# An mLSTM scan with a gated MLP: every store on SyncE's queue, and another order of work ahead of the first step

## The chip, the cores and the metric

The kernel runs on one core of one Trainium2 chip. The metric is the device time of one execution in microseconds (us); lower is better. The median of the runs shown stands for the kernel. Beside them there is one profiled execution, from which all durations below are read.

## What is computed

The inputs are q, k, v and an output gate of shape (4, 8, 768, 40), and an input and a forget gate of shape (4, 8, 768): 4 batches, 8 heads, 768 positions, 40 features. The reference is a stabilised recurrence over the positions, followed by a two-layer MLP:

```python
for t in range(S):
    m_new = np.maximum(f_gate[:, :, t] + m, i_gate[:, :, t])
    f_stab = np.exp(f_gate[:, :, t] + m - m_new)
    i_stab = np.exp(i_gate[:, :, t] - m_new)
    C = f_stab * C + i_stab * einsum('bhd,bhe->bhde', v[t], k[t])
    n = f_stab * n + i_stab * k[t]
    y[t] = sigmoid(o_gate[t]) * einsum('bhde,bhe->bhd', C, q[t]) / max(|n.q[t]|, 1)
x = y as (3072, 320)
h = x @ w_in                      # (320, 2048)
out = (h * sigmoid(h)) @ w_out    # (2048, 320)
```

(The indices are shortened here.) Everything is in 32-bit floats; the two weights come in as 64-bit words.

## The kernel before, in words

**Units.** The recurrence is cut into 12 chunks of 64 positions. A unit (class `Unit`) is one chunk of two batches, all heads: 24 units, numbered in the order of time, two for each chunk. A unit computes 64 by 64 scores of q and k (`scores`, L511), multiplies them with a matrix of decay factors in tile D (`weigh`, L538), applies them to v (`values`, L567, or `near_values` and `far_values`, L583 and L598), adds what earlier chunks left in the state Cm, and updates the state: `keys` (L530) multiplies k by the last decay factors, `state` (L648) multiplies that with v, `carry` (L666 for the first chunk, L668 and L674 later) adds it to Cm. The result is divided by its norm (`norm`, `level`, L611 to L621), multiplied by the output gate (`gate` makes the tanh, L488; `scale`, L635, makes tile x), transposed on TensorE (`xpose`, L690) and put into the MLP's input (`xput`, L696 to L702).

**Steps.** Three units make a step of 384 tokens (class `Step`): 8 steps. A step runs over 16 blocks of 128 hidden features, fc = 0 to 15. `mm1(fc)` is x times w_in (L743, tile ph); `act(fc)` makes the gated value: a tanh on ScalarE (L750, tile th), a product on VectorE (L764), and in steps 1 to 7 a split into two parts (gh on ScalarE, L769; gl on VectorE, L773). `mm2(fc)` adds that block's product with w_out (L794) into three accumulators `pout`, one for each 128 tokens. `mm2` runs two blocks behind `mm1`, so the last two blocks of a step run beside blocks 0 and 1 of the next one. After the last `mm2` of each accumulator `store` (L804 to L818) evicts it on ScalarE (L814, tile ob) and issues two DMAs of 64 rows each to the output (L818).

**Order.** All engines run a hand-written order: what stands first in the program is issued first on its engine, and every engine and DMA queue is in order. In each step the three units of the next one are worked into the blocks: unit u starts at block 2, 7 or 12 (`PLACES`). At that block TensorE runs the unit's matmuls after `mm1` (`block`), one block later `turn` transposes its x and issues the loads of a later unit on SyncE's queue: D, qk, ko, vb (L430 to L451) and lq (L464).

**Queues.** Loads go through SyncE's queue. A store goes through SyncE's queue in steps 0 and 1 and for the first half of each store of the last step, and through ScalarE's queue in all other cases (L817). Two writes of the running log-decay to a scratch tensor LFd go through ScalarE's queue (`spread`, L185).

**Ahead of the first step.** Units 0, 1 and 2 are computed by an order of their own (L857 to L955): the gate recurrence for the first two chunks on VectorE, the decay factors of these units by matmuls (`mask`, `expo`, `reach`) and exponentials on ScalarE, then scores, values, state and x of each. Beside it, weights are loaded in pieces, `Part`: i0 to i7 (256 columns of w_in, its first 256 rows), c0 to c6 (512 columns of w_in's last 64 rows), o0 to o7 (256 rows of w_out). `wmake` turns a piece from 64-bit words into 32-bit floats by two ScalarE passes (L259, L260) and one on VectorE (L261) and then issues the load of a later piece. `halve` (L274) splits a c piece: for each of two halves, a copy on ScalarE (L280) and a subtraction (L281), on VectorE unless another engine is named. In step 0 the table `FILL` adds work after each block: the rest of the weights' pieces, unit 3's remainder, and the rest of the gate recurrence. Unit 3's first work on GpSimd is `near` (L495), a product that waits for its qk.

Of the kernel before, what the change touches and what calls it, by code (L numbers as in the profile page):

```python
# [8 lines left out]
F32 = mybir.dt.float32  # L9
# [5 lines left out]
ALU = mybir.AluOpType  # L15
# [3 lines left out]
B, H, S, D = 4, 8, 768, 40  # L19
L = 64  # L20
# [3 lines left out]
DM = H * D  # L24
# [4 lines left out]
NT = UPS * UT  # L29
NSTEP = NU // UPS  # L30
# [13 lines left out]
def mlstm_mlp_kernel(  # L44
# [113 lines left out]
    def gates(lo, hi):  # L158

        init = NEG if lo == 0 else m_t[:, lo - 1 : lo]  # L160
        nc.vector.tensor_tensor_scan(
            m_t[:, lo:hi], f_t[:, lo:hi], i_t[:, lo:hi], init, op0=ALU.add, op1=ALU.max
        )
        yield
        l1 = max(lo, 1)
        tt = nc.vector.tensor_tensor
        tt(out=f_t[:, l1:hi], in0=f_t[:, l1:hi], in1=m_t[:, l1 - 1 : hi - 1], op=ALU.add)
        yield
        tt(out=f_t[:, l1:hi], in0=f_t[:, l1:hi], in1=m_t[:, l1:hi], op=ALU.subtract)
# [46 lines left out]
    class Part:  # L216
# [54 lines left out]
                nc.vector.tensor_copy(wi[self.lo], full)  # L271
            self.full = full

        def halve(self, eng=None):  # L274
            K, n, full = self.K, self.n, self.full
            for k in range(2):
                a, b = slice(k * K, (k + 1) * K), slice((1 - k) * K, (2 - k) * K)
                cs = slice(k * n, (k + 1) * n)
                hi = self.hi[a, :, cs]
                nc.scalar.copy(hi, full[a])  # L280
                (eng or nc.vector).tensor_tensor(  # L281
                    out=self.hi[b, :, cs], in0=full[a], in1=hi.bitcast(F32), op=ALU.subtract
                )

    def split_out(i):

# [31 lines left out]
        )  # L318


    order = "i0 c0 i1 o0 i2 c2 o1 i3 o2 c4 i4 o3 i5 o4 c6 i6 o5 i7 o6 o7"
    parts = [part(x[0], int(x[1])) for x in order.split()]
    nload, nmade = [0], [0]

    def halve(i, eng=None):
        next(p for p in parts if p.nm == f"c{i}").halve(eng)

    def wload(n):
        for p in parts[nload[0] : nload[0] + n]:
            p.load()  # L330
        nload[0] = min(nload[0] + n, len(parts))

    def wmake(n):

        for p in parts[nmade[0] : nmade[0] + n]:
            p.make()
            wload(1)
        nmade[0] = min(nmade[0] + n, len(parts))
# [16 lines left out]
    def couple(name):  # L355

        return psP.tile([128, H, 128], F32, tag="p", name=name)

    class Unit:


        def __init__(self, n):
            self.n, self.c, self.p = n, n // NP, n % NP


        def mask(self, to=None):
# [120 lines left out]
        def gate(self):  # L487
            nc.scalar.activation(self.ot, self.ot, AF.Tanh, scale=0.5)  # L488

        def look(self):  # L490
            nc.scalar.activation(self.lq, self.lq, AF.Exp)  # L491

# [28 lines left out]
            self.last = p2.tile([128, H], F32, tag="last", name=f"last{self.n}")  # L521
            nc.scalar.copy(self.last, self.Dm[:, :, L - 1])

        def keys(self):
            last = getattr(self, "last", None)
            if last is None:
                last = self.Dm[:, :, L - 1]
            if self.c < NC - 1:
                self.kw = p2.tile([128, H, D], F32, tag="kw", name=f"kw{self.n}")
                nc.vector.tensor_tensor(  # L530
                    out=self.kw,
                    in0=self.kt,
                    in1=last.unsqueeze(2).broadcast_to([128, H, D]),
                    op=ALU.mult,
                )
# [80 lines left out]
            nc.vector.reciprocal(den, den)  # L616
            self.den = den

        def level(self):
            y = self.po[:, :, :D]  # L620
            nc.vector.tensor_tensor(  # L621
                out=y, in0=y, in1=self.den.unsqueeze(2).broadcast_to([128, H, D]), op=ALU.mult
            )

        def scale(self):
            n, y = self.n, self.po[:, :, :D]
# [3 lines left out]
            for to, e in (  # L630
                (xf[:, : H * DA].rearrange("p (h e) -> p h e", e=DA), slice(0, DA)),
                (rest[:, 0], slice(DA, D)),
                (rest[:, 1], slice(DA, D)),
            ):
                nc.vector.scalar_tensor_tensor(  # L635
                    out=to, in0=self.ot[:, :, e], scalar=1.0, in1=y[:, :, e],
                    op0=ALU.add, op1=ALU.mult,
                )
# [67 lines left out]
    class Step:  # L706
# [97 lines left out]
        def store(self, t):  # L804
            n = self.j * UPS + t
            c, p = n // NP, n % NP
            if self.j < NSTEP - 1:
                ob = p3.tile([128, DM], F32, tag="ob", name=f"ob{n}")
            else:
                ob = pb.tile([128, DM], F32, tag="big", name=f"ob{n}")  # L810
            if self.j == NSTEP - 1 and t == UPS - 1:
                nc.vector.tensor_scalar(ob, self.po[t], 0.5, None, op0=ALU.mult)
            else:
                nc.scalar.activation(ob, self.po[t], AF.Copy, scale=0.5)  # L814
            for k in range(2):
                r = (2 * p + k) * S + c * L
                q = nc.sync if self.j in (0, 1) or self.j == NSTEP - 1 and k == 0 else nc.scalar  # L817
                q.dma_start(out[r : r + L, :], ob[k * L : (k + 1) * L])  # L818


# [55 lines left out]
    for _ in range(2):  # L876
# [4 lines left out]
    run(5, gates(0, L))  # L881
    thirds(0)
    widen()
    run(5, gates(L, 2 * L))
# [4 lines left out]
    u0.scores()  # L889
    warm(1)  # L890
    u0.mask()
    u0.expo()
    u0.expo_act()
    u1.mask()
    u1.expo()
    u1.expo_act()
    u0.keys()
    u0.weigh()
    u2.reach()
    u2.reach_act()  # L900
    u0.gate()
    u2.mask()
    u2.expo()
    u2.expo_act()
    u2.keep()
    u2.near()
    warm(1)
    u1.scores()
    u1.keys()
    u1.weigh()  # L910
    u0.place()
    u0.values()
    u0.state()
    u0.carry()
    u1.gate()
    u0.norm()
    u0.level()
    u2.scores()
    u2.weigh()
    u1.place()  # L920
    u1.values()
    u2.place()
    u2.values()
    u2.gate()
    u0.scale()
    u1.norm()
    u1.level()
    u2.norm()
    u2.level()
    u2.scale()  # L930
    u1.scale()
    wmake(2)
    steps[0] = st = Step(0)
    u2.keys()
    u0.xpose()
    u1.state()
    u1.carry()
    u3.reach()
    u3.mask(couple("e3")[:, :4, :].rearrange("p b (c t) -> p (b c) t", t=L))
    u3.expo()  # L940
    u2.room(psU, "u")
    u2.xpose()
    u1.xpose()
    u0.xput(st)
    halve(0, nc.gpsimd)
    u2.xput(st)
    u1.xput(st)
    u3.load_qk()
    u3.load_kvo()
    u2.state()  # L950
    u3.reach_act()
    u3.near()
    run(5, two)
    wmake(1)
    u3.expo_act()  # L955
    FILL = {
        0: lambda: (run(1, near), wmake(1), u2.carry(), u3.gate(), u3.keys()),
        1: lambda: (wmake(1), u3.scores(), u3.weigh(), u4.load_qk(), u4.load_kvo()),
        2: lambda: (wmake(2), run(2, near), u4.load_d(), u4.load_q(), u4.shift()),
        3: lambda: (halve(2), wmake(1), u4.add(), run(1, late[0])),  # L960
# [34 lines left out]
    for j in range(NSTEP):  # L995
        st = steps[j]
# [105 lines left out]
```

## Time and profile before

| | us |
|---|---|
| median of 3 runs | 464.67 (464.63 to 466.96) |
| the profiled execution, device time | 465.99 |
| its span, first to last instruction | 464.1 |
| TensorE's matmul busy in it | 445.1 |
| first `mm1` of step 0 starts | 23.93 |
| `mm1(2)` of steps 2, 3, 4, 5, 6, 7 starts | 144.28, 196.51, 253.11, 307.83, 361.56, 414.85 |

A row of the timeline gives the start in us from the span's start, the duration, the engine, the line, the operation, the tile written and those read, shapes, the number of like instructions merged into the row, and in brackets how long the engine was idle before it and what ended that. PE is TensorE's matmul, PEld its weight load, DVE is VectorE, ACT ScalarE, POOL GpSimd, SP SyncE; a q behind a name is that engine's queue of DMA issues. A row of the windows view gives a stretch, its length, then for each engine its busy time in it and the number of instructions, then TensorE's granted clock (1.00 is full speed), the DMA engines' busy share and GB/s. In the waits view a row gives who waited for whom, the total, how often, and the longest.

### The profile page before, as it was taken

The page shows a single profiled execution, that of the slowest core. Times are in us where ns is not written, and L with a number is a line of the kernel's source. Part 1 is how long each engine was busy: PE and PEld are TensorE (multiplying, and loading weights), DVE is VectorE, ACT ScalarE, POOL GpSimd, SP SyncE. Part 2 cuts the span into 40 slices and gives each one's busy share as a digit, 9 for nine tenths or more (in the row PEclk, how much of TensorE's full clock was granted, in tenths as well). Part 3 has the DMA queues.
Part 4 walks back from the last instruction along what each step waited for, and adds up shares of the span by engine and source line. Part 5 has one row for each costly group of instructions (what it writes and reads, how often), then busy time and mean ns, then how long its engine had stood idle before and what let it go on. Part 6 is the DMA issues. An engine that isn't in the chain of part 4 may idle for free.

```text
span 464.1 us, 11033 instructions
## 1 busy us (share of the span) xinstructions
PE 445.1 (96%) x4477; PEld 408.8 (88%) x4477; DVE 269.8 (58%) x609; ACT 212.1 (46%) x442; POOL 115.6 (25%) x123
## 2 busy tenths in 40 slices
PE   7899999999999999979999899998999899999995
PEld 3667677899999999979999799998999799998995
DVE  5777799578775566444664555636655355533342
ACT  6674856444753442525424344434344344333332
POOL 4224234134142234131431332322332311000000
PEclk9899999999999999998999999999999999998999
DMA  8999896361331442141430522413313200001001
GB/s 211 320 295 274 235 265 148 97 159 49 81 122 40 127 122 65 59 110 56 124 101 22 148 63 76 123 48 118 122 31 93 62 1 2 2 12 32 0 1 42
DMA packets 27314, 47.03 MB, mean 101 GB/s; under 512 B 4160, under 2 KB 14464, under 8 KB 27264
## 3 DMA queue, kind: packets, MB, share of 16 engines
q1 hardware_dynamic: 24224, 43.45, 33.6%
q10 hardware_dynamic: 3040, 2.89, 2.3%
q8 instruction: 35, 0.57, 0.5%
q14 instruction: 15, 0.12, 0.1%
HBM read 42.30 MB, written 4.01 MB: 100 GB/s over the span
## 4 chain that ended last, share of the span: by engine, by line
PE 83%; DMA 6%; DVE 3%; ACTq 3%; ACT 2%; issue 1%; SPq 0%; DVEq 0%
PE ph L743 37%; PE pout L794 35%; DMA wro<-in_w_out_dram 3%; ACTq L818 3%; PE p L598 3%; DMA qk<-in_qk_dram 3%; PE p L511 2%; PE pu L648 2%; PE p L583 2%; PE p L690 2%; ACT ob L814 1%; ACT th L750 1%; DVE th L764 1%; DVE D L538 1%; PE pt L193 0%
## 5 line engine op out<-in xcount | busy, mean ns | idle before, releaser
L750 ACT ACTIVATE th<-ph 128x384 f32<-128x384 f32 x128 | 62.4, 487 | 139.8 <-PE ph L743 132.7
L764 DVE SCALAR_TENSOR_TENSOR th<-th,ph 128x384 f32<-128x384 f32 x112 | 62.1, 555 | 107.5 <-ACT th L750 106.9
L743 PE MATMUL ph<-xh,wh 128*128 128x384 f32 x336 | 116.3, 346 | 0.0
L743 PE MATMUL ph<-xl,wh 128*128 128x384 f32 x336 | 114.6, 341 | 0.0
L794 PE MATMUL pout<-woh,gh 128*128 128x320 f32 x336 | 106.5, 317 | 2.2 <-ACT ob L814 2.2
L794 PE MATMUL pout<-woh,gl 128*128 128x320 f32 x336 | 104.2, 310 | 0.0
L794 PE MATMUL pout<-wol,gh 128*128 128x320 f32 x336 | 103.7, 308 | 0.0
L773 DVE TENSOR_TENSOR gl<-th,gh 128x384 fp32r<-128x384 f32 x112 | 64.6, 577 | 47.5 <-ACT gh L769 47.5
L769 ACT CAST gh<-th 128x384 fp32r<-128x384 f32 x112 | 57.5, 513 | 74.9 <-DVE th L764 74.3
L743 PE MATMUL ph<-xh,wl 128*128 128x384 f32 x224 | 76.6, 342 | 0.0
L794 PEld LDWEIGHTS pout<-woh,gh 128*128 128x128 f32 x336 | 63.6, 189 | 5.5 <-ACT ob L814 3.4
L495 POOL TENSOR_TENSOR qt<-qk,lq 104x512 f32<-104x512 f32 x22 | 29.5, 1340 | 141.5 <-ACT lq L491 125.0
L743 PEld LDWEIGHTS ph<-xl,wh 128*128 128x128 f32 x336 | 63.8, 190 | 0.2
L743 PEld LDWEIGHTS ph<-xh,wh 128*128 128x128 f32 x336 | 63.7, 190 | 0.2
L794 PEld LDWEIGHTS pout<-wol,gh 128*128 128x128 f32 x336 | 63.5, 189 | 0.0
L794 PEld LDWEIGHTS pout<-woh,gl 128*128 128x128 f32 x336 | 63.5, 189 | 0.0
L668 POOL TENSOR_TENSOR Cm<-Cm,lq 40x328 f32<-40x328 f32 x40 | 30.2, 756 | 114.5 <-PE p L598 113.0
L743 PEld LDWEIGHTS ph<-xh,wl 128*128 128x128 f32 x224 | 42.6, 190 | 0.0
L794 PE MATMUL pout<-wo,g 128*128 128x320 f32 x96 | 28.8, 436 | 0.6 <-DVE wo L261 0.6
L482 POOL TENSOR_TENSOR D<-D,am 128x512 f32<-128x512 f32 x20 | 25.8, 1288 | 7.4 <-DMA D<-LFd 5.4
L474 POOL TENSOR_TENSOR am<-mask,aT 128x512 f32<-128x512 f32 x20 | 23.2, 1160 | 7.8 <-DVE aT L203 6.3
L743 PE MATMUL ph<-x,wi 128*128 128x384 f32 x64 | 23.8, 494 | 0.0
(113 smaller groups left out, 485.6 us busy)
## 6 DMA issues: line engine op xcount, KB each, us to landing
qk<-in_qk_dram SPq DMA_DIRECT2D x24, 416.0 KB
ko<-in_ko_dram SPq DMA_DIRECT2D x24, 320.0 KB
wro<-in_w_out_dram SPq DMA_DIRECT2D x8, 640.0 KB
D<-LFd SPq DMA_DIRECT2D x40, 128.0 KB
wri<-in_w_in_dram SPq DMA_DIRECT2D x8, 512.0 KB
vb<-in_vp_dram SPq DMA_DIRECT2D x48, 82.0 KB
out_dram<-ob ACTq DMA_DIRECT2D x33, 80.0 KB
lq<-LFd SPq DMA_DIRECT2D x20, 128.0 KB
```

Of the source, the lines that this page charges most:

```text
L474: nc.gpsimd.tensor_tensor(out=self.am, in0=mask.unsqueeze(1).broadcast_to([128, H, L]), in1=aT[:, self.c, self.p, :].unsqueeze(2).broadcas ...
L482: nc.gpsimd.tensor_tensor(out=self.Dm, in0=self.Dm, in1=self.am, op=ALU.add)
L495: nc.gpsimd.tensor_tensor(out=self.qt, in0=self.q, in1=self.lq, op=ALU.mult)
L598: nc.tensor.matmul(self.out[g * L : (g + 1) * L, d, :, e, :], self.qt[:, j, :], cm[:, :, j, :], start=False, stop=True, skip_group_check=True,
L668: nc.gpsimd.tensor_tensor(out=v, in0=v, in1=self.lq[r, :, L - 1].unsqueeze(2).broadcast_to([D, H, D1]), op=ALU.mult,)
L743: nc.tensor.matmul(ph, w, x, start=(i == 0), stop=(i == len(ops) - 1))
L750: nc.scalar.activation(th, ph, AF.Tanh, scale=0.5)
L764: nc.vector.scalar_tensor_tensor(out=th, in0=th, scalar=1.0, in1=ph, op0=ALU.add, op1=ALU.mult)
L769: nc.scalar.copy(gh, th)
L773: nc.vector.tensor_tensor(out=gl, in0=th, in1=gh.bitcast(F32), op=ALU.subtract)
L794: nc.tensor.matmul(self.po[t], g[:, ts], w, start=(fc == 0 and i == 0), stop=(last and i == len(ops) - 1),)
L818: q.dma_start(out[r : r + L, :], ob[k * L : (k + 1) * L])
```

## The change

Four things change.

1. **Stores.** Every store of steps 0 to 6 is issued on SyncE's queue. The last step is as before.
2. **Ahead of the first step** the order is another. Units 0 and 1 get their decay factors and keys before the second chunk's gate recurrence. `keys` of units 0, 1 and 2 run on GpSimd. Unit 0's normalised result goes into an SBUF tile (`level(aside=True)`), and its x is made on GpSimd: `open` adds 1 to the gate's tanh, and `scale` then multiplies three times. Unit 3's `near` moves into step 0's block 0.
3. **The piece c0** (tail rows of w_in) is loaded and made ahead of i0, and its split runs in two phases, first both copies on ScalarE, later both subtractions, on VectorE where they were on GpSimd.
4. **The piece i1** is made in step 0's block 0, where it was made ahead of the step.

```diff
-        def halve(self, eng=None):
+        def halve(self, eng=None, phases=(0, 1)):
...
-    order = "i0 c0 i1 o0 i2 c2 o1 i3 o2 c4 i4 o3 i5 o4 c6 i6 o5 i7 o6 o7"
+    order = "c0 i0 i1 o0 i2 c2 o1 i3 o2 c4 i4 o3 i5 o4 c6 i6 o5 i7 o6 o7"
...
+        def open(self):
+            self.opened = True
+            nc.gpsimd.tensor_scalar(self.ot, self.ot, 1.0, None, op0=ALU.add)
...
-        def keys(self):
+        def keys(self, eng=nc.vector):
...
-        def level(self):
-            y = self.po[:, :, :D]
+        def level(self, aside=False):
+            y = self.y = self.po[:, :, :D]
+            if aside:
+                t = p2.tile([128, NT], F32, tag="th", name=f"y{self.n}")
+                self.y = t[:, :DM].rearrange("p (h e) -> p h e", e=D)
...
+                if self.opened:
+                    nc.gpsimd.tensor_tensor(
+                        out=to, in0=self.ot[:, :, e], in1=y[:, :, e], op=ALU.mult
+                    )
+                    continue
...
-                q = nc.sync if self.j in (0, 1) or self.j == NSTEP - 1 and k == 0 else nc.scalar
+                q = nc.sync if self.j < NSTEP - 1 or k == 0 else nc.scalar
```

The order ahead of the first step, after the change, from where it differs (`run(5, gates(L, 2 * L))` is the second chunk's recurrence):

```python
    u0.scores()
    warm(1)
    u0.mask(); u0.expo(); u0.expo_act(); u0.keys(nc.gpsimd)
    u1.mask(); u1.expo(); u1.expo_act(); u1.keys(nc.gpsimd)
    run(5, gates(L, 2 * L))
    thirds(1)
    ...
    u0.weigh(); u2.reach(); u2.reach_act(); u2.near(); u2.mask()
    u1.scores(); u1.weigh(); u0.place(); u0.values()
    u2.expo(); u2.expo_act(); u2.keep()
    u0.gate(); u0.open(); u0.state(); u0.carry()
    u2.scores(); u0.norm(); u0.level(aside=True); u0.scale()
    u2.weigh(); u1.place(); u1.values(); u1.gate(); u2.gate()
    u1.norm(); u1.level(); u2.place(); u2.values()
    u0.room(); u0.xpose(); u1.state()
    u3.mask(...); u3.expo()
    wmake(1)
    u2.norm(); u1.scale(); u2.level(); u2.scale(); u2.keys(nc.gpsimd)
    steps[0] = st = Step(0)
    u0.xput(st)
    halve(0, None, [0]); wmake(1); halve(0, None, [1])
    u1.xpose(); u3.reach(); u2.room(psU, "u"); u2.xpose(); u2.state()
    u1.xput(st); u2.xput(st)
    u3.expo_act(); u1.carry(); u3.reach_act()
    u3.load_qk(); u3.load_kvo()
    run(5, two)
    FILL = {
        0: lambda: (wmake(1), u3.near(), run(1, near), wmake(1),
                    u2.carry(), u3.gate(), u3.keys()),
        ...
```

(Several calls are put on one line here. `run(1, near)` issues the first write to LFd.)

More of the change, by code (lines that the diff above doesn't have):

```diff
@@ L272, in make @@
             self.full = full
-        def halve(self, eng=None):
+        def halve(self, eng=None, phases=(0, 1)):
             K, n, full = self.K, self.n, self.full
[L276 to L283, printed above, removed]
+            for phase in phases:
+                for k in range(2):
+                    a, b = slice(k * K, (k + 1) * K), slice((1 - k) * K, (2 - k) * K)
+                    cs = slice(k * n, (k + 1) * n)
+                    hi = self.hi[a, :, cs]
+                    if phase == 0:
+                        nc.scalar.copy(hi, full[a])
+                        continue
+                    (eng or nc.vector).tensor_tensor(
+                        out=self.hi[b, :, cs], in0=full[a], in1=hi.bitcast(F32), op=ALU.subtract
+                    )
     def split_out(i):
@@ L318, in part, with halve @@
         )
-    order = "i0 c0 i1 o0 i2 c2 o1 i3 o2 c4 i4 o3 i5 o4 c6 i6 o5 i7 o6 o7"
+    order = "c0 i0 i1 o0 i2 c2 o1 i3 o2 c4 i4 o3 i5 o4 c6 i6 o5 i7 o6 o7"
     parts = [part(x[0], int(x[1])) for x in order.split()]
     nload, nmade = [0], [0]
-    def halve(i, eng=None):
-        next(p for p in parts if p.nm == f"c{i}").halve(eng)
+    def halve(i, *args):
+        next(p for p in parts if p.nm == f"c{i}").halve(*args)
     def wload(n):
@@ L363, in __init__ @@
             self.n, self.c, self.p = n, n // NP, n % NP
+            self.opened = False
         def mask(self, to=None):
@@ L529, in keys @@
                 self.kw = p2.tile([128, H, D], F32, tag="kw", name=f"kw{self.n}")
-                nc.vector.tensor_tensor(
+                eng.tensor_tensor(
                     out=self.kw,
@@ L617, in norm @@
             self.den = den
-        def level(self):
-            y = self.po[:, :, :D]
+        def level(self, aside=False):
[3 more added lines that the diff above has]
+                self.y = t[:, :DM].rearrange("p (h e) -> p h e", e=D)
             nc.vector.tensor_tensor(
-                out=y, in0=y, in1=self.den.unsqueeze(2).broadcast_to([128, H, D]), op=ALU.mult
+                out=self.y, in0=y, in1=self.den.unsqueeze(2).broadcast_to([128, H, D]), op=ALU.mult
             )
         def scale(self):
-            n, y = self.n, self.po[:, :, :D]
+            n, y = self.n, self.y
             self.x = p2.tile([128, 3, 128], F32, tag="x", name=f"x{n}")
@@ L634, in scale @@
             ):
+                if self.opened:
+                    nc.gpsimd.tensor_tensor(
+                        out=to, in0=self.ot[:, :, e], in1=y[:, :, e], op=ALU.mult
+                    )
+                    continue
                 nc.vector.scalar_tensor_tensor(
@@ L883, in mlstm_mlp_kernel @@
     widen()
+    u0.scores()
+    warm(1)
+    u0.mask()
+    u0.expo()
+    u0.expo_act()
+    u0.keys(nc.gpsimd)
+    u1.mask()
+    u1.expo()
+    u1.expo_act()
+    u1.keys(nc.gpsimd)
     run(5, gates(L, 2 * L))
@@ L888, in mlstm_mlp_kernel @@
     late = [gates(4 * L, 8 * L), gates(8 * L, S)]
[L889 to L897, printed above, removed]
     u0.weigh()
@@ L900, in mlstm_mlp_kernel @@
     u2.reach_act()
-    u0.gate()
+    u2.near()
     u2.mask()
+    u1.scores()
+    u1.weigh()
+    u0.place()
+    u0.values()
     u2.expo()
@@ L905, in mlstm_mlp_kernel @@
     u2.keep()
[L906 to L912, printed above, removed]
+    u0.gate()
+    u0.open()
     u0.state()
     u0.carry()
-    u1.gate()
+    u2.scores()
     u0.norm()
-    u0.level()
-    u2.scores()
+    u0.level(aside=True)
+    u0.scale()
     u2.weigh()
@@ L921, in mlstm_mlp_kernel @@
     u1.values()
+    u1.gate()
+    u2.gate()
+    u1.norm()
+    u1.level()
     u2.place()
     u2.values()
[L924 to L927, printed above, removed]
+    u0.room()
+    u0.xpose()
+    u1.state()
+    u3.mask(couple("e3")[:, :4, :].rearrange("p b (c t) -> p (b c) t", t=L))
+    u3.expo()
+    wmake(1)
     u2.norm()
+    u1.scale()
     u2.level()
     u2.scale()
-    u1.scale()
-    wmake(2)
+    u2.keys(nc.gpsimd)
     steps[0] = st = Step(0)
[L934 to L937, printed above, removed]
+    u0.xput(st)
+    halve(0, None, [0])
+    wmake(1)
+    halve(0, None, [1])
+    u1.xpose()
     u3.reach()
-    u3.mask(couple("e3")[:, :4, :].rearrange("p b (c t) -> p (b c) t", t=L))
-    u3.expo()
     u2.room(psU, "u")
     u2.xpose()
-    u1.xpose()
-    u0.xput(st)
-    halve(0, nc.gpsimd)
+    u2.state()
+    u1.xput(st)
     u2.xput(st)
-    u1.xput(st)
+    u3.expo_act()
+    u1.carry()
+    u3.reach_act()
     u3.load_qk()
     u3.load_kvo()
-    u2.state()
-    u3.reach_act()
-    u3.near()
     run(5, two)
-    wmake(1)
-    u3.expo_act()
     FILL = {
-        0: lambda: (run(1, near), wmake(1), u2.carry(), u3.gate(), u3.keys()),
+        0: lambda: (
+            wmake(1),
+            u3.near(),
+            run(1, near),
+            wmake(1),
+            u2.carry(),
+            u3.gate(),
+            u3.keys(),
+        ),
         1: lambda: (wmake(1), u3.scores(), u3.weigh(), u4.load_qk(), u4.load_kvo()),
```

## The prediction

> **What bounds the kernel now.** I read the page first, then a table of windows, one for each step from the start of its `mm1(2)` to that of the next step's.
>
> ```profile
> span 464.1 us, 11033 instructions
> ```
>
> ```profile
> 144.28:196.51 52.23, 52.23 (x572) 50.97 (x570) 30.45 (x69) 22.11 (x47) 15.95 (x15) 1.00 0.33 91
> 196.51:253.11 56.60, 54.16 (x572) 52.47 (x570) 30.11 (x69) 22.32 (x47) 15.74 (x15) 0.97 0.29 84
> 253.11:307.83 54.72, 52.87 (x572) 51.09 (x571) 30.04 (x69) 22.22 (x48) 15.75 (x15) 1.00 0.31 87
> 307.83:361.56 53.73, 52.50 (x572) 50.98 (x571) 29.62 (x67) 22.13 (x48) 15.75 (x15) 1.00 0.30 89
> 361.56:414.85 53.29, 51.18 (x506) 49.45 (x506) 25.82 (x60) 20.52 (x44) 6.41 (x6) 1.00 0.06 15
> ```
>
> TensorE is the bound, and in step 2 it has no idle time at all: 52.23 busy of 52.23. Steps 3, 4 and 5 run the same 572 matmuls and take 56.60, 54.72 and 53.73. So the question is what holds TensorE in the later steps. The waits view of TensorE from 207 to 420 us names it:
>
> ```profile
> PE p L690 <- DVE x L635: 7.1, 4, 2.4
> PE pout L794 <- ACT ob L814: 2.2, 4, 1.0
> ```
>
> The first is the transpose of a unit's x, the second an accumulator that waits to be evicted. The timeline at the head of step 3 shows where both begin:
>
> ```profile
> 197.45 1.19 ACTq L818 DMA_DIRECT2D out_dram<-ob  x2
> ...
> 198.76 0.44 ACT L814 ACTIVATE ob<-pout 128x320 f32<-128x320 f32 x1 [1.34 <-PE ph L743]
> ...
> 199.22 1.10 SPq L430 DMA_DIRECT2D D<-LFd  x2
> ...
> 201.41 1.89 ACTq L818 DMA_DIRECT2D out_dram<-ob  x2
> ...
> 203.35 0.49 ACT L750 ACTIVATE th<-ph 128x384 f32<-128x384 f32 x1 [1.97 <-DMA out_dram<-ob]
> ...
> 207.28 0.55 PE L690 MATMUL p<-ident,x 128*128 128x128 f32 x3 [2.44 <-DVE x L635]
> ```
>
> ScalarE stands idle while its own queue issues the stores: an eviction, two issues, an eviction, two issues, and so on. The tanh `th` of the next block waits behind them until 203.35. VectorE needs `th` before it can go on to the unit's norm and x, and TensorE waits 2.44 for that x. The wait that ends last is ScalarE's queue. At the head of step 2 the stores are on SyncE's queue already:
>
> ```profile
> 144.76 1.08 ACT L814 ACTIVATE ob<-pout 128x320 f32<-128x320 f32 x3
> ...
> 145.22 4.82 SPq L818 DMA_DIRECT2D out_dram<-ob  x6
> ...
> 145.96 0.49 ACT L750 ACTIVATE th<-ph 128x384 f32<-128x384 f32 x1
> ...
> 150.12 1.19 SPq L430 DMA_DIRECT2D D<-LFd  x2
> ...
> 152.55 0.42 PE L743 MATMUL ph<-xh,wh 128*128 128x384 f32 x1
> ```
>
> Three evictions follow each other in 1.08, `th` starts at 145.96, 1.68 after the step's mark, where in step 3 it is 6.84. That is the same structure with the changed queue, measured in this very trace.
>
> **Part 1: the stores of steps 2 to 6.** I take step 2 as the price of a boundary whose stores are on SyncE. Losses by the windows: 56.60 - 52.23 = 4.37, 54.72 - 52.23 = 2.49, 53.73 - 52.23 = 1.50. Steps 6 and 7 have fewer matmuls, so I compare stretches. From `mm1(2)` to `mm1(4)` step 2 takes 152.55 - 144.28 = 8.27. For steps 6 and 7 the chain view has:
>
> ```profile
> 372.48 0.53 PE ph L743 x3
> ...
> 424.03 1.39 PE ph L743 x8
> ...
> 426.73 1.41 PE ph L743 x8
> ...
> 429.46 1.41 PE ph L743 x8
> ```
>
> Step 6: 372.48 - 361.56 = 10.92, a loss of 2.65. Step 7 has no unit in these blocks; two blocks of 429.46 - 426.73 = 2.73 would take 5.46, and it takes 424.03 - 414.85 = 9.18, a loss of 3.72. The sum is 4.37 + 2.49 + 1.50 + 2.65 + 3.72 = 14.73. Part of it is the clock:
>
> ```profile
> 207.95:211.36 3.41, 3.41 (x14) 3.41 (x13) 2.34 (x5) 1.38 (x3) 0.00 (x0) 0.50 0.68 207
> ...
> 416.17:419.58 3.41, 1.74 (x10) 1.22 (x9) 0.00 (x0) 0.87 (x2) 0.00 (x0) 1.00 0.39 96
> 419.58:422.99 3.41, 3.41 (x14) 3.41 (x12) 1.15 (x3) 1.49 (x3) 0.00 (x0) 0.50 0.19 48
> ```
>
> Twice the granted clock was 0.50 for 3.41, which costs 1.7 each time; 7.1 + 2.2 of waits and 3.4 of clock make 12.7, and about 2 is restart.
>
> What moves to SyncE: six issues a boundary. Behind them in its queue stand the next loads: D's come 5.84 after the mark in step 2 (150.12) and 2.71 in step 3 (199.22), so 3.1 later. The cover is that these loads are for a unit three places ahead, about a step of time; step 2 had the same delay and no idle. What is late next? In step 7 nothing hides ScalarE's 1.08 of evictions, but `mm2` stands two blocks, 5.46, behind `mm1`. I take -14.7; bounds -12.7 (only the waits and the clock) to -15.
>
> **Part 2: ahead of the first step.** These rows carry it:
>
> ```profile
> 10.59 0.49 DVE L530 TENSOR_TENSOR kw<-ko,D 128x320 f32<-128x320 f32 x1 [0.67 <-ACT D L394]
> ...
> 14.00 1.30 POOL L495 TENSOR_TENSOR qt<-qk,lq 104x512 f32<-104x512 f32 x1 [7.35 <-DMA qk<-in_qk_dram]
> ...
> 15.42 0.67 DVE L635 SCALAR_TENSOR_TENSOR x<-ko,po 128x256 f32<-128x256 f32 x3
> ...
> 21.09 1.52 POOL L281 TENSOR_TENSOR wh<-wtc,wh 64x256 fp32r<-64x256 f32 x2 [5.79 <-ACT wh L280]
> ...
> 22.94 0.29 DVE L702 TENSOR_TENSOR xb<-px,xb 128x128 fp32r<-128x128 f32 x1 [1.83 <-ACT xb L701]
> ...
> 23.93 1.56 PE L743 MATMUL ph<-x,wi 128*128 128x384 f32 x4
> ```
>
> VectorE loses three keys, 3 x 0.49, and unit 0's x, 0.67; it gains the two subtractions that GpSimd did in 1.52. GpSimd gains three keys, an `open` and three products. By its rows (0.76 for 256 columns, 1.30 for 512, so 2.5 to 3.0 ns a column) keys and `open` are 0.8 to 1.0 each and unit 0's 384 columns 1.0 to 1.2. `open` stands behind unit 2's `near`, which waits for its qk until 14.00 as before and ends at 15.30; so unit 0's x is ready at 15.30 + 0.9 + 1.1 = 17.3. That is about 1.2 later than VectorE's 16.09, but not last: unit 2's values need the same `near`, and its norm and x follow. The keys have their covers: those of units 0 and 1 end before 14, unit 2's before its `state`. What the new order can win is VectorE's 1.83 of idle time before the last `xput`s. I put the first `mm1` 1.8 earlier, at about 22.1; bounds 0 and 2.5.
>
> Whether this reaches the end is decided at the first `mm2`:
>
> ```profile
> 13.87 6.88 DMA wro<-in_w_out_dram
> ```
>
> ```profile
> 25.87 0.49 ACT L750 ACTIVATE th<-ph 128x384 f32<-128x384 f32 x1
> ...
> 27.11 1.11 SPq L451 DMA_DIRECT2D vb<-in_vp_dram  x2
> ...
> 27.72 0.38 ACTq L185 DMA_DIRECT2D LFd<-home  x1
> 28.14 0.79 ACT L259 ACTIVATE wro<-wro 128x640 f32<-128x640 f32 x1 [1.78 <-DMA wro<-in_w_out_dram]
> ...
> 29.13 0.47 SPq L239 DMA_DIRECT2D wrc<-in_w_in_dram  x1
> ...
> 30.52 1.88 PE L794 MATMUL pout<-wo,g 128*128 128x320 f32 x6 [0.59 <-DVE wo L261]
> ```
>
> The timeline says that ScalarE waited for the weights o0 until 28.14. But o0's load was issued at 13.87 and the chain has its landing at 20.75. What stands between 26.36 and 28.14 on ScalarE is the issue of the LFd write at 27.72. I infer that this issue waits for the landing of an earlier load, and that SyncE's issues around it, at 27.11 and 29.13, do the same; the loads keep their order, bar c0, and their rate. After the change the issue still stands ahead of o0's make. With `mm1(0)` 1.8 earlier and i1's make between, ScalarE comes to it at about 25.9, and then waits until 27.7, or 27.1 if its turn falls one issue earlier. From the first pass over o0 to the matmul it is 30.52 - 28.14 = 2.38, so `mm2(0)` starts at 29.9 to 30.5. The gain ahead of the step is then eaten: 0 to 0.6, and I take 0.4. If the issue does not wait, it starts at 28.3 and 2.2 is won. i1's make in block 0 is hidden: `mm1(2)` needs it, and that stands before the same wait. c0 ahead of i0 moves only which of the two lands first. The later `halve`s have the same instructions.
>
> **The sum.** -14.7 - 0.4 = -15.1. The profiled execution took 465.99 (span 464.1 and 1.9 around it), so 450.9 for it; it stands 1.3 above the median of 464.67, and I forecast a median of 449.6.
>
> **A rule against the change.** The keys on GpSimd run beside VectorE's gate recurrence. What such company costs is bounded by the row of the key products themselves, whose inputs lie in SBUF and which run beside GpSimd's work all through the kernel:
>
> ```profile
> L530 DVE TENSOR_TENSOR kw<-ko,D x21: 472/484/957, 10.6 to 340.7; 128x320 f32<-128x320 f32 x21
> ```
>
> The median is 0.484, the worst 0.957, so 0.5 an operation at most; that is inside the bounds of the first `mm1`. The Trainium skill, "SBUF — State Buffer", section "SBUF: two separate sides", says that VectorE's operations with two SBUF inputs and GpSimd's share a port pair as a lock, and that the loser waits out the whole instruction. By that rule three keys would hold VectorE up by 0.8 to 1.0 each, the first `mm1` would gain nothing, and the sum would be 450.0 instead of 449.6; no row of this trace shows a product held up so long.
>
> **The rivals.**
>
> - *B: the start comes through.* The LFd issue falls behind other loads and does not wait. For: o0 is there at 20.75. Against: SyncE's issues at 27.11 and 29.13 stand on both sides of it. -14.7 - 2.2: 447.8.
> - *C: the start gets dearer.* TensorE is earlier but waits 2.4 for o0 instead of 0.59, and the clock drops as at 419.58, after only 1.67 idle in 3.41; that costs 1.7. -14.7 + 1.7: 451.7; with the LFd issue two places later in the queue, at 29.13 instead of 27.72, 1.4 more: 453.1. "TensorE: Matmul & The Clock Gate" of the Trainium skill, section "What's actually happening", has the drop after an idle window of 3.4; by that C's clock term would vanish, but the row at 416.17, busy 1.74 of 3.41, is followed by the drop, so the trace does not agree.
> - *D: half stays.* VectorE's own chain (norm, x) takes over as TensorE's wait at each boundary. For: the wait is named after it. Against: no idle in step 2. -7.3: 457.4.
> - *E: slower.* SyncE's queue makes the loads late. D comes 3.1 later at each boundary, and as the queue is in order all three units of a step can inherit it: 12 units in steps 3 to 6. At half of 3.1 each, 12 x 1.6 = 19.2 against the 15.1 won: 468.8. It decides from the point where a unit waits 1.3 for its loads (15.1 / 12). Against: step 2 with the same delay has no idle.
>
> **How the numbers follow.** A 0.55, B 0.20, C 0.17, D 0.05, E 0.03. The time is A's, 449.6. The range reaches from B less 1.0 (the bound of part 1 and a start that gains more) to C's dearer end plus 0.9 (the spread of runs): 446.8 to 454.0, and leaves D and E out. About 0.5% of the time, 2.3, is what a measurement can tell from none. A to D are faster by more: 0.96 with a little of D taken off; E is slower: 0.03; the rest 0.01.
>
> **What would show it.** Right: every window from step 2 to 6 at 52.2 (step 6 at 50.6), no wait of L690 for L635, no 0.50 clock after 30, ScalarE's `th` within 2 of each mark. Part 2 right: the first `mm1` near 22.1, `mm2(0)` near 30, ScalarE idle before L185. Wrong: windows still above 53, a wait of L430's readers for D, or a first `mm1` after 23.9.

## The result, and the profile after

| | before | after |
|---|---|---|
| median, us | 464.93 of 4 runs (464.63 to 466.96) | 452.16 of 4 runs (451.68 to 452.19) |
| profiled execution | 465.99, span 464.1 | 452.14, span 450.4 |
| first `mm1` of step 0 | 23.93 | 22.23 |
| first `mm2` of step 0 | 30.52 | 31.18 |
| `mm1(2)` of step 2 | 144.28 | 144.96 |

The ratio is 0.9714, with a 95% interval of 0.9685 to 0.9743. The forecast was 449.6, in a range of 446.8 to 454.0: the sign and the range hold, and the time is 2.6 higher. Slow executions, more than 1.5% above the fastest of their kernel, are left out of the medians and ranges here and below: 469.19 of the order alone, 484.64 of the stores in four DMAs, and one of 2432.45 of the kernel before.

The windows of the kernel after, from `mm1(2)` of each step to that of the next, the last one to the end of the span (columns as before; the third number is TensorE's busy time):

```profile
144.96:197.19 52.23, 52.23 (x572) 50.97 (x570) 30.46 (x69) 22.12 (x47) 15.94 (x15) 1.00 0.34 91
197.19:249.47 52.28, 52.28 (x572) 51.02 (x571) 30.46 (x69) 22.11 (x47) 15.93 (x15) 1.00 0.34 91
249.47:301.69 52.22, 52.22 (x572) 50.96 (x570) 30.45 (x69) 22.12 (x47) 15.94 (x15) 1.00 0.34 91
301.69:353.96 52.27, 52.27 (x571) 51.01 (x570) 30.05 (x68) 22.10 (x47) 15.93 (x15) 1.00 0.34 91
353.96:404.64 50.68, 50.68 (x507) 49.45 (x506) 26.26 (x61) 20.54 (x43) 6.61 (x6) 1.00 0.06 16
404.64:450.40 45.76, 40.98 (x258) 40.71 (x256) 16.66 (x31) 16.45 (x34) 0.00 (x0) 0.98 0.09 22
```

Length and busy time are equal in steps 2 to 6: TensorE has no idle time left there, and the granted clock is 1.00. Against the windows of before, steps 3 to 7 save 4.32, 2.50, 1.46, 2.61 and 3.49 (the last from 464.1 - 414.85 = 49.25), together 14.38. Up to the mark of step 2 the kernel is 144.96 - 144.28 = 0.68 later. 14.38 - 0.68 is the whole difference of the spans, 13.7.

The head of step 3 in the timeline of after, ScalarE first and then SyncE's queue:

```profile
197.67 1.08 ACT L830 ACTIVATE ob<-pout 128x320 f32<-128x320 f32 x3
198.87 0.49 ACT L766 ACTIVATE th<-ph 128x384 f32<-128x384 f32 x1
```

```profile
198.13 5.01 SPq L834 DMA_DIRECT2D out_dram<-ob  x6
203.23 1.18 SPq L434 DMA_DIRECT2D D<-LFd  x2
```

The tanh comes 198.87 - 197.19 = 1.68 after the mark, where it came 6.84 after it. The six issues take 5.01 of SyncE's queue instead, with D's loads behind them.

The start, rows of ScalarE, then VectorE, then TensorE:

```profile
25.12 0.66 ACT L260 ACTIVATE wri<-wri 128x512 uint32<-128x512 uint8 x1
28.45 0.33 ACTq L185 DMA_DIRECT2D LFd<-home  x1
28.83 0.79 ACT L259 ACTIVATE wro<-wro 128x640 f32<-128x640 f32 x1 [3.04 <-DMA wro<-in_w_out_dram]
```

```profile
30.30 0.83 DVE L261 SCALAR_TENSOR_TENSOR wo<-wro 128x640 uint32<-128x640 uint32 x1 [3.67 <-ACT wro L260]
```

```profile
22.23 1.56 PE L759 MATMUL ph<-x,wi 128*128 128x384 f32 x4
...
27.07 0.69 PE L519 MATMUL p<-qk 40*64 40x64 f32 x32 [1.29 <-DMA qk<-in_qk_dram]
...
31.18 1.88 PE L810 MATMUL pout<-wo,g 128*128 128x320 f32 x6 [1.58 <-DVE wo L261]
```

ScalarE has nothing to do from 25.78 to 28.45, then issues the LFd write, and only then makes o0, for which TensorE waits 1.58. The timeline names o0's load for those 3.04, as it did before; the prediction held that it was the issue in front. The chain view of after has a different load ahead of that issue, the second half of unit 3's vb:

```profile
19.76 8.62 DMA vb<-in_vp_dram
28.38 0.02 issue
...
28.45 0.33 ACTq L185
```

Which of the two it was is settled by the experiments.

### The profile page after: what moved, and what is told of

Read it like the earlier page. It is cut to its first block, busy times and chain, and to the rows that moved or that the text cites. A ratio compares the mean times of both kernels' runs of the same rounds, so it can differ in the third digit from the quotient of the medians.

```text
span 450.4 us, 11053 instructions
## 1 busy us (share of the span) xinstructions
PE 439.4 (98%) x4476; PEld 405.7 (90%) x4476; DVE 272.0 (60%) x605; ACT 211.4 (47%) x442; POOL 119.2 (26%) x128
## 4 chain that ended last, share of the span: by engine, by line
PE 92%; DMA 5%; SPq 1%; ACT 0%; issue 0%; ACTq 0%; DVE 0%
PE ph L759 40%; PE pout L810 39%; PE p L606 3%; PE p L519 3%; PE pu L664 2%; PE p L591 2%; DMA vb<-in_vp_dram 2%; DMA wri<-in_w_in_dram 2%; DMA ko<-in_ko_dram 2%; PE p L706 2%; PE pt L193 0%; SPq L455 0%; SPq L442 0%; ACT ob L830 0%; DVE wo L261 0%
## 5 line engine op out<-in xcount | busy, mean ns | idle before, releaser
L810 PE MATMUL pout<-woh,gh 128*128 128x320 f32 x336 | 105.4, 314 | 0.0
L789 DVE TENSOR_TENSOR gl<-th,gh 128x384 fp32r<-128x384 f32 x112 | 65.6, 586 | 47.5 <-ACT gh L785 47.5
L546 DVE TENSOR_TENSOR D<-p,D 128x512 f32<-128x512 f32 x24 | 16.5, 689 | 14.1 <-PE p L606 10.6
```

The source lines that it names most:

```text
L546: nc.vector.tensor_tensor(out=self.Dm, in0=self.ps, in1=self.Dm, op=ALU.mult)
L789: nc.vector.tensor_tensor(out=gl, in0=th, in1=gh.bitcast(F32), op=ALU.subtract)
L810: nc.tensor.matmul(self.po[t], g[:, ts], w, start=(fc == 0 and i == 0), stop=(last and i == len(ops) - 1),)
```

## The experiments

**The stores alone.** The kernel before, with one line of the change:

```diff
-                q = nc.sync if self.j in (0, 1) or self.j == NSTEP - 1 and k == 0 else nc.scalar
+                q = nc.sync if self.j < NSTEP - 1 or k == 0 else nc.scalar
```

> The kernel before with only the stores of steps 2 to 6 moved to SyncE's queue. Theory (the whole gain is the stores; the new order ahead of the first step costs 0.7): 14.4 us less than before, a span near 449.7, the first mm1 at 23.9 and mm2(0) at 30.5 as before, no TensorE idle over 0.1 us after 31. Rival (the new order carries part of the gain): slower than the changed kernel, a span over 450.4.

453.81 (451.80 to 454.53), ratio 0.9735 (0.9687 to 0.9784). From `mm1(2)` of step 2 to the end its profile takes 305.4, as after does, so the store line alone brings the whole gain at the heads. The 449.7 was missed at the start. Two rows of TensorE in this kernel:

```profile
18.84 0.50 PE L567 MATMUL po<-vb,D 128*64 128x82 f32 x7 [2.62 <-issue]
...
26.36 2.23 PE L743 MATMUL ph<-x,wi 128*128 128x384 f32 x4
```

TensorE stands idle for 2.62 in the middle of unit 2's values, waiting for nothing that the profile names, and the first `mm1` comes at 26.36 instead of 23.93. No edit of this kernel reaches there. After the stall the granted clock was 0.50 from 20.94 to 27.77, for 6.83, where before had it for 3.41. `mm2(0)` starts at 33.09. The last section returns to this stall.

**The order alone.** The kernel after, with the old store line (the same diff, the other way round):

> The changed kernel with the old store queues. Theory: the start costs 0.7 us, so the span is 464.1 + 0.7 = 464.8, with mm2(0) at 31.2 and the same waits of about 9 us at the heads of steps 3 to 7. Rival (the order is worth something): under 464.1.

465.23 (461.32 to 467.33), ratio 0.9993 (0.9955 to 1.0032): without the stores the new order is worth nothing that can be measured. The executions lie 6.0 apart, and a gain of 1 to 2 would not show among them. Its windows from step 2 on:

```profile
145.62:197.84 52.22, 52.22 (x571) 50.96 (x570) 30.46 (x69) 22.12 (x47) 15.93 (x15) 1.00 0.35 91
197.84:252.72 54.88, 52.47 (x572) 50.95 (x570) 30.04 (x69) 22.12 (x47) 15.72 (x15) 1.00 0.29 87
252.72:306.86 54.14, 52.44 (x571) 50.93 (x570) 30.02 (x69) 22.12 (x47) 15.73 (x15) 1.00 0.32 88
306.86:360.58 53.72, 52.46 (x571) 50.95 (x570) 29.63 (x68) 22.12 (x47) 15.72 (x15) 1.00 0.31 89
360.58:413.44 52.86, 51.15 (x508) 49.41 (x506) 25.85 (x61) 20.53 (x43) 6.39 (x6) 1.00 0.06 15
413.44:461.30 47.86, 41.51 (x258) 40.72 (x256) 16.59 (x31) 16.57 (x34) 0.00 (x0) 0.99 0.08 21
```

In this execution the clock is 1.00 in all of steps 2 to 6, with the same waits at the heads. Against after, steps 3 to 7 lose 2.60, 1.92, 1.45, 2.18 and 2.10, together 10.2, where the profile of before lost 14.4. The rest of that profile's loss was in good part the two drops of the clock, 1.7 each.

**Both again, side by side.** After and the stores alone once more, without an edit, beside each other on another chip.

> The changed kernel once more, beside the stores-only kernel on the same chip, because the start of single executions differed by up to 2.6 us: TensorE stood idle 0 to 2.6 us in unit 2's values, and so the 0.7 by which the profiles put the new order behind is inside that scatter. Theory: 452.2, as at first. If the order of the start wins anything by the median, this lies below the stores-only kernel by more than 1; if it costs the 0.7 that the two first profiles gave (mm2(0) at 31.18 against 30.52), it lies above it by 0.7.

> The kernel before with only the stores' queue changed, a second time. Theory (the order of the start is worth nothing by the median): within 1 of the changed kernel in the same call, about 452. Rival (the order wins about what the medians of the other call had, 453.8 against 451.8 and 452.3 of two kernels with the new order): 453.5 to 454. Rival (the order costs 0.7): 451.5.

After: 451.89 (451.43 to 452.53), ratio 0.9704 (0.9677 to 0.9730). The stores alone: 453.66 (452.00 to 454.65), ratio 0.9736 (0.9709 to 0.9764). Of 11 runs of the stores alone, 7 lie above the slowest of 9 runs of after (452.53). So with the stores moved, the new order wins about 1.7 by the medians (the intervals of the two ratios overlap), though the first profiles had it 0.7 behind. The profile of before showed a start without the stall. In the second profile of the stores alone the stall is there again, and the first `mm1` comes at 24.68:

```profile
18.85 0.50 PE L567 MATMUL po<-vb,D 128*64 128x82 f32 x7 [1.13 <-issue]
```

From step 2's mark on, this profile takes 305.4 too, so it is the start that differs. In the three profiles with the old start (before, and the stores alone twice) `mm2(0)` comes at 30.52, 33.09 and 31.70. In the seven that have the new start with its keys on GpSimd and the LFd write in its place it comes at 30.90 to 31.85. Before's 30.52 was an early one of its kind, and the 0.66 by which after's profile lies behind it is less than the scatter.

**The LFd write later.** In the kernel after, its issue is moved from block 0, ahead of o0's make, to block 1, behind i2's:

```diff
         0: lambda: (
             wmake(1),
             u3.near(),
-            run(1, near),
             wmake(1),
...
-        1: lambda: (wmake(1), u3.scores(), ...),
+        1: lambda: (wmake(1), run(1, near), u3.scores(), ...),
```

> The changed kernel with the first LFd write moved on ScalarE from ahead of o0's make in block 0 to behind i2's make in block 1. Theory (ScalarE's queue stands at that issue until a load has landed, while o0 is there since 21.8): o0 is made from 25.8 on, mm2(0) starts at the end of mm1(2), near 29.3 instead of 31.2, and the span falls by 1.9 to 448.5. Rival (o0 has not landed before 28.8): mm2(0) stays at 31.2 and the span at 450.4.

451.77 (450.68 to 452.81), ratio 0.9703 (0.9651 to 0.9755). On ScalarE and TensorE:

```profile
25.11 0.66 ACT L260 ACTIVATE wri<-wri 128x512 uint32<-128x512 uint8 x1
25.66 0.79 ACT L259 ACTIVATE wro<-wro 128x640 f32<-128x640 f32 x1
...
27.97 0.33 ACTq L185 DMA_DIRECT2D LFd<-home  x1
```

```profile
28.93 1.24 PE L810 MATMUL pout<-wo,g 128*128 128x320 f32 x4
30.62 0.78 PE L810 MATMUL pout<-wo,g 128*128 128x320 f32 x2 [0.45 <-DVE Cm L690]
...
51.88 1.56 PE L759 MATMUL ph<-x,wi 128*128 128x384 f32 x4 [0.78 <-DVE wi L261]
```

o0 is made at 25.66 with no idle time in front, and `mm2(0)` starts 2.25 earlier. So o0's data had been there, and it was the LFd issue that ScalarE stood behind. The issue itself waits for a landing. Its completion semaphore is the one that the second half of unit 3's vb has, eight DMAs earlier. In twelve of the fourteen profiles the issue starts 0.07 to 0.08 behind that half's landing (28.38 and 28.45 in after, 27.64 and 27.72 in before). This run is one of them, though the issue stands elsewhere in the order. In the other two it comes later. Part of the gain is given back: 0.45 at once, and 0.78 at 51.88, where piece i4 is late. The span is 449.5, 0.9 less than after's, where 1.9 less was expected.

**i0 loaded first again.** The kernel after, with i0's load issued ahead of c0's; both are still made in the new order:

```diff
+    loads = [parts[1], parts[0], *parts[2:]]
...
-        for p in parts[nload[0] : nload[0] + n]:
+        for p in loads[nload[0] : nload[0] + n]:
```

> The changed kernel with i0's load issued ahead of c0's as before; c0 is still made first. Theory (two small transfers ahead of a large one leave the DMA engines short of work while the next issue waits, so all later loads land about 0.9 later): the load that holds the LFd write lands at 27.7 instead of 28.4, mm2(0) starts at 30.5, the span is 449.7. Rival (the order of these loads does not matter, the lateness comes from unit 3's ko, which waits for GpSimd): mm2(0) stays at 31.2.

452.33 (451.24 to 453.18), ratio 0.9711 (0.9665 to 0.9758): no difference. The vb load in front of the LFd write landed at 28.26, not at 27.7, and `mm2(0)` came at 31.10, not at 30.5: the order of these two loads is not what makes the others late. Its profile had 2.03 of the unnamed stall, so its first `mm1`, at 23.23, says nothing on the loads.

**Three of six issues on ScalarE.** The kernel after, with the second DMA of each store of steps 2 to 6 on ScalarE:

```diff
-                q = nc.sync if self.j < NSTEP - 1 or k == 0 else nc.scalar
+                q = nc.sync if self.j in (0, 1) or k == 0 else nc.scalar
```

> The changed kernel, but the second DMA of each store of steps 2 to 6 is issued on ScalarE again: 15 of 30 issues come back. Theory (a chain: ScalarE's issues push the next tanh back, and TensorE loses only what goes beyond its cover at that head): with three issues instead of six the tanh is about half as late, 1.68 + 5.2 / 2 = 4.3 after the mark instead of 6.84, so each head's loss falls by about 2.6: from 4.37, 2.49, 1.50, 2.65, 3.72 to 1.8, 0, 0, 0, 1.1, in sum 2.9: 455.1. Rival 1 (every issue on ScalarE costs the same, 14.4 / 30 = 0.48): 15 x 0.48 = 7.2, 459.4. Rival 2 (the issue waits for a landing, so one is as bad as two): nearly all of 14.4, above 463.

452.93 (451.51 to 453.77), ratio 0.9726 (0.9700 to 0.9752). Step 3's window and the last one:

```profile
197.10:249.37 52.27, 52.27 (x571) 51.01 (x570) 30.02 (x69) 22.25 (x47) 16.04 (x15) 1.00 0.33 91
...
404.55:451.10 46.55, 41.49 (x258) 40.70 (x256) 16.60 (x31) 16.68 (x34) 0.00 (x0) 0.98 0.08 22
```

With the tanh at 201.02, 3.92 after the mark, step 3 loses nothing, nor do 4, 5 and 6. Only step 7 loses 46.55 - 45.76 = 0.79, where my theory had 2.9 lost in steps 3 and 7 (455.1). An equal price for each issue (459.4) is ruled out.

**Five of six.** Only the first store's first half stays on SyncE:

```diff
-                q = nc.sync if self.j < NSTEP - 1 or k == 0 else nc.scalar
+                q = nc.sync if self.j in (0, 1) or k == 0 and (t == 0 or self.j == NSTEP - 1) else nc.scalar
```

> The changed kernel, with five of the six stores' issues of each of steps 2 to 6 on ScalarE, the first one on SyncE. With three the tanh came 3.92 after the mark instead of 1.68 and steps 3 to 6 lost nothing; with six it came at 6.84 and they lost 4.4 to 1.5. Theory (cover of at least 2.2 at each head, beyond it TensorE loses one for one): with five the first pair frees ScalarE 0.5 earlier, but the third pair still waits until 4.43 for its accumulator, so the tanh comes at about 6.3 to 6.8 and nearly all is lost: 12 to 14, median 464. Rival 1 (each issue on ScalarE costs the same): 25 x 0.48 = 12, 464. Rival 2 (what counts is how long ScalarE stands in the first two pairs): the tanh at about 5.4, and the losses 3 to 7, median 455 to 459.

459.34 (458.35 to 462.02), ratio 0.9861 (0.9821 to 0.9902). ScalarE at the head of step 3, that step's window, and TensorE's waits from 140 on:

```profile
201.26 0.44 ACT L830 ACTIVATE ob<-pout 128x320 f32<-128x320 f32 x1 [1.21 <-PE p L591]
201.73 1.14 ACTq L834 DMA_DIRECT2D out_dram<-ob  x2
202.92 0.49 ACT L766 ACTIVATE th<-ph 128x384 f32<-128x384 f32 x1 [1.21 <-PE pu L664]
```

```profile
198.01:251.44 53.43, 52.48 (x572) 50.97 (x570) 30.27 (x69) 22.23 (x47) 15.75 (x15) 1.00 0.31 89
```

```profile
PE p L706 <- DVE x L651: 3.8, 4, 0.9
PE pout L810 <- ACT ob L830: 1.0, 1, 1.0
```

The tanh is at 202.92 - 198.01 = 4.91, and the old waits are back at a smaller size: steps 3 to 6 lose 1.15 each, step 7 1.78. My own theory (464) fell, since the third eviction does not wait until 4.43 here but comes at 3.25. The second rival, with a loss of 3 to 7, was right: the sum is 6.4. The runs put step 3 on one curve: tanh at 1.68 and 3.92, no loss; at 4.91, 1.15; at 6.65, in the run of the order alone, 2.60. If the loss beyond the cover is one for one, the two late points have the cover end at 3.76 and 4.05, and at 3.92 there was still no loss: about 4.

**Stores in four DMAs on SyncE.** The kernel after, each store of steps 1 to 6 in four DMAs of 32 rows:

```diff
-                q.dma_start(out[r : r + L, :], ob[k * L : (k + 1) * L])
+                w = L if self.j in (0, NSTEP - 1) else L // 2
+                for h in range(0, L, w):
+                    q.dma_start(out[r + h : r + h + w, :], ob[k * L + h : k * L + h + w])
```

> The changed kernel, with each store of steps 1 to 6 issued on SyncE as four DMAs of 32 rows instead of two of 64: 12 issues at a boundary instead of 6, about 10 us of SyncE's queue instead of 5, so the loads of D, qk, ko, vb and lq behind them come about 5 us later still. Theory (the loads are for a unit about a step of time ahead, so they have slack): no loss, 452.2 within 0.7, every window from step 2 on as in the changed kernel (52.2). Rival (the prediction's case E: SyncE is at its limit): 1 to 2.5 us at each of six boundaries, 458 to 467, with a wait for D or qk behind a head.

451.90 (451.02 to 454.87), ratio 0.9713 (0.9682 to 0.9744). SyncE's queue at the head of step 3, and that step's window:

```profile
197.82 6.31 SPq L836 DMA_DIRECT2D out_dram<-ob  x12
204.23 1.22 SPq L434 DMA_DIRECT2D D<-LFd  x2
```

```profile
196.88:249.16 52.28, 52.28 (x572) 51.02 (x571) 30.47 (x69) 22.13 (x47) 15.95 (x15) 1.00 0.34 91
```

Twelve issues took 6.31, not the 10 that I had expected, so D's loads come only 1.3 later than in after, measured from the mark (7.35 against 6.04). There is no loss. How late they may come was not reached.

**The keys and x on VectorE.** The kernel after in its new order, with the three keys and unit 0's x back on VectorE:

```diff
-    u0.keys(nc.gpsimd)
+    u0.keys()
...
-    u0.open()
```

(The keys of units 1 and 2 likewise.)

> The changed kernel's order, with the three keys and unit 0's x back on VectorE (no open), so that GpSimd has only near. By the medians the new start is worth 1.8 (451.9 against 453.7 with the stores alone on the same chip). Theory (the order wins it, not the engines): VectorE has 2.1 more work ahead of the first mm1, part of it in gaps, and no company of GpSimd's keys (the cast that took 0.77 takes 0.21), so the first mm1 within 0.5 of 22.2 and the median within 0.5 of 452. Rival G (the work taken off VectorE wins it): first mm1 at 23.5 or later, 453.2 to 454. Rival L (GpSimd's keys hold VectorE up by more than they take off): first mm1 at 21.5, 451.2.

458.02 (457.71 to 459.56), ratio 0.9838 (0.9796 to 0.9880): 6 slower than after, where the theory had 452 and the worst rival 454. VectorE, and the first `mm1`:

```profile
8.74 0.49 DVE L538 TENSOR_TENSOR kw<-ko,D 128x320 f32<-128x320 f32 x1 [1.70 <-ACT D L398]
11.18 0.49 DVE L538 TENSOR_TENSOR kw<-ko,D 128x320 f32<-128x320 f32 x1 [1.95 <-DMA ko<-in_ko_dram]
11.59 0.33 DVE L161 TENSOR_TENSOR_SCAN home<-home 32x64 f32<-32x64 f32 x1
...
14.47 0.69 DVE L546 TENSOR_TENSOR D<-p,D 128x512 f32<-128x512 f32 x1
```

```profile
26.76 1.56 PE L759 MATMUL ph<-x,wi 128*128 128x384 f32 x4
```

The new order has the keys ahead of the second chunk's recurrence. On VectorE's in-order queue unit 1's key waits for its ko until 11.18, and the recurrence waits behind it; unit 0's weigh comes at 14.47, where after has it at 10.49. The first `mm1` is 4.5 later than in after, and `mm2(0)`, at 36.62, 5.4 later. So order and engine belong together: the keys can stand that early because a queue of their own does the waiting. Unit 0's x was moved in the same run; its share is not measured.

**LFd and i4 both moved.** The kernel with the LFd write later, and i4 made ahead of c4's halves in block 6:

```diff
-        6: lambda: (halve(4), wmake(2), run(1, late[0])),
+        6: lambda: (wmake(1), halve(4), wmake(1), run(1, late[0])),
```

> Two moves in step 0 of the changed kernel: the LFd write from block 0 to block 1, behind i2's make, as in the run before, and i4's make ahead of c4's halves in block 6. Theory (the LFd issue costs 2.2 at mm2(0), and the 0.78 given back at 51.88 is i4 being made late): mm2(0) near 28.9, no wait for i4, so 1.7 less than the changed kernel's profile: span 448.8, median 450.5. Rival (what is won at mm2(0) is lost again wherever the next load is late, since the start is bound by loads): another wait of 0.5 to 1.7 before 80 us, median 451.5 to 452.2.

450.57 (449.57 to 451.62), ratio 0.9667 (0.9630 to 0.9705), span 448.4: as expected, and with the next run the fastest. `mm2(0)` starts at 28.79, the wait for i4 is gone, and `mm1(2)` of step 2 comes at 143.02 instead of 144.96. The ratio's interval overlaps that of after; the 2.0 of span are placed by the trace.

**Unit 3's scores later as well.** As the last one, with unit 3's near moved to block 1 and its scores and weigh to block 2:

```diff
-            u3.near(),
...
-        1: lambda: (wmake(1), run(1, near), u3.scores(), u3.weigh(), u4.load_qk(), u4.load_kvo()),
-        2: lambda: (wmake(2), run(2, near), ...),
+        1: lambda: (wmake(1), u3.near(), run(1, near), u4.load_qk(), u4.load_kvo()),
+        2: lambda: (u3.scores(), u3.weigh(), wmake(2), run(2, near), ...),
```

> As the kernel with the LFd write and i4's make moved, and unit 3's near in block 1, its scores and weigh in block 2, behind mm2(0). There TensorE no longer waits for unit 3's qk ahead of mm1(2) (0.8 to 1.5), and o0's last pass on VectorE (1.36 with near beside it on GpSimd) takes its 0.83. Theory: mm2(0) 0.5 earlier, at 28.4, 0.5 less in all: median 450.0. Rival (o0's making bounds mm2(0), and the moved work makes the next piece late): same as the other within 0.3, or a wait in blocks 2 to 4 of 0.5 to 1.

450.50 (449.75 to 452.08), ratio 0.9670 (0.9633 to 0.9708): no further gain. TensorE's wait changes its name:

```profile
27.02 1.56 PE L759 MATMUL ph<-x,wi 128*128 128x384 f32 x4 [0.99 <-DVE wi L261]
...
28.92 1.88 PE L810 MATMUL pout<-wo,g 128*128 128x320 f32 x6
```

It no longer waits for unit 3's qk but for i1, and `mm2(0)` stands where it stood.

## Why the prediction was right, and where its numbers were off

**Part 1, the stores: the mechanism right, the size that of one execution.** Between the two profiled executions step 2 was the price of a head with its stores on SyncE to within 0.05 in each of steps 3 to 5, and the sum is 14.38 against 14.73. Step 7 kept 0.23 less than reckoned. The mechanism, ScalarE's queue holding the tanh back until VectorE's x is late for TensorE, is shown by the runs with three and five issues: it has a threshold, and neither rival D (7.3 stays) nor E (SyncE too late) came. The profile of the run with five issues is a small copy of before's waits view. But over many executions the store line is worth less than between these two. Alone it has a ratio of 0.9735 and 0.9736 on two chips, which is 12.3 (11.0 to 13.5 by the second's interval), and the profile of the order alone, with the old store line and no drop of the clock in steps 2 to 6, loses 10.2. The 14.7 had 3.4 from two clock drops in it.

**From profile to median: the step that failed most.** The prediction took the profiled execution as 1.3 above the median throughout and took the same 1.3 off the result. The profiled run after (452.14) stands at its median (452.16): the excess did not carry over, and that is half of the 2.6. In executions of before the time goes with the clock. Of the 38 that were measured beside the experiments, the nine with a mean granted clock of 0.985 took 466.9 to 469.2, and the three with 0.996 took 462.5 to 463.9. The profiled one had 0.989, with two of its drops at heads whose waits the change removes; after has none from step 2 to step 6. How many drops the median execution of before has, and where, no profile shows. This miss and the 12.3 above are probably one thing seen from two sides; they are not to be added.

**Part 2, the first `mm1`: right.** 22.1 forecast, 22.23 measured. VectorE's 1.83 of idle time ahead of the last `xput`s is gone in after. Ten profiles with the new order and its keys on GpSimd have the first `mm1` at 21.67 to 23.75, three with the old start at 23.93 to 26.36.

**Part 2, the first `mm2`: mis-sized.** The cause was as the prediction put it: ScalarE idle ahead of the LFd issue, o0 already there. The run with the issue moved shows it. But the issue was put at 27.1 to 27.7 and came at 28.45. The load that it waits for, the second half of unit 3's vb, landed at 28.38, where it landed at 27.64 before; the prediction had the loads keep their times. Between the two profiles the term was -0.4 and measured +0.66, which is 1.1 of the 2.6. What makes the loads 0.7 later was not settled; the order of c0 and i0 is not it. And the +0.66 is itself a difference of two single starts. By the medians of the two kernels run side by side, the new start wins 1.8 with the stores moved, more than the 0.4 that was taken.

**Luck.** By the medians, then, the stores were put about 2.4 too high and the start about 1.4 too low. The two misses pull against each other. That the sum of -15.1 comes within 1.5 of what the change wins on that chip (465.46 to 451.89, 13.6) is in part luck.

**The rivals.** B (the LFd issue does not wait) and C's clock drop ahead of `mm2` did not happen; C's later issue did, with 0.73 instead of 1.4, and TensorE's wait for o0 was 1.58 instead of C's 2.4.

**The rule on the shared port.** What the Trainium skill says in "SBUF — State Buffer", section "SBUF: two separate sides", is seen in after, where a VectorE product at 41.23 takes 1.49 beside a GpSimd product of 1.36 (0.41 in before), and once more in the run with the keys on VectorE, where the first two rows are VectorE's and the third is GpSimd's:

```profile
28.34 0.28 DVE L167 TENSOR_TENSOR home<-home 32x128 f32<-32x128 f32 x1
28.65 1.39 DVE L169 TENSOR_TENSOR home<-home 32x128 f32<-32x128 f32 x1
```

```profile
28.63 1.28 POOL L503 TENSOR_TENSOR qt<-qk,lq 104x512 f32<-104x512 f32 x1 [11.46 <-ACT lq L427]
```

A product that takes 0.28 takes 1.39 and ends 0.13 after GpSimd's. The prediction's sentence that no product is held up so long holds for the trace of before alone. In after a cast of 0.21 takes 0.77 beside unit 0's key; before has one of 0.77 too, at 5.29, beside GpSimd's memsets. The price that the prediction worked out from the rule, all of the gain at the first `mm1`, was not paid: the key's company costs 0.56 there once, and the first `mm1` still came 1.7 earlier.

## What to carry to other kernels

In this kernel the DMA issues on an engine that also computes cost nothing up to the cover of that engine's next result, about 4 at step 3's head, and about one for one beyond it. Find an identical stage elsewhere in the same trace whose issues are on another queue, and use it as the price. When the profiled execution is above the median, ask whether the excess lies in the stalls that the change removes, before carrying it over to the result, and take a second profile before a start of 30 us is judged by one. An instruction that may wait for a transfer, a DMA issue included, belongs behind the work that is due next on its engine, or on a queue where nothing stands behind it.

## What the runs showed of the hardware

**A stall that no wait names.** In six profiles TensorE stood idle in the middle of unit 2's values with "issue" as the only reason: 2.62 (the stores alone), 1.43 (the order alone), 2.03 (i0 first), 1.13 (the stores again), 0.30 (LFd and i4) and 0.87 (unit 3's scores later). It stops each time ahead of the same matmul: behind the ninth of unit 2's last sixteen in the two profiles with the old start, behind the tenth in the four with the new one. In the traces one 16,384-byte packet of the queue "q8 instruction" lies near it. Where that packet ended at 17.49, 16.69, 17.16, 17.48, 15.56 and 15.92, TensorE went on at 18.84, 18.08, 18.62, 18.85, 16.89 and 17.38, which is 1.33 to 1.46 later each time. In none of the fourteen profiles does that matmul start sooner behind the packet: in before it ended at 14.86 and the matmul came at 16.27, in its turn, and after the 13.59 of the LFd write later it came at 17.61. The DMA engines were busy throughout just before the longest stall: the first row below, of the stores alone, has a share of 1.05. I take it that TensorE waits for its next instructions, which come late among the weights' loads; no run moved that packet, and what sets its start, 12.38 to 19.79 in fourteen profiles, stays open. The idle time differs by up to 2.62 between single executions, more than the effect of the order that was to be judged. Not all of it reaches the end: with 2.03 of it, the run with i0 first had its `mm2(0)` at 31.10, and after, with no such wait named, at 31.18.

```profile
14.00:17.50 3.50, 2.22 (x73) 2.06 (x74) 2.79 (x10) 2.60 (x6) 0.70 (x1) 1.00 1.05 330
```

```profile
12.06:15.48 3.42, 3.42 (x51) 2.70 (x50) 1.73 (x5) 1.22 (x4) 1.27 (x1) 0.50 0.98 263
```

The second row, of after, is the only stretch but for the last 1.4 us in which after's granted clock was 0.50. Before had it at 20.22 too, beside the two that the prediction quotes.
